# Attention and a squared-ReLU layer on one core: the up-projection by 128-token blocks, with the first loads reordered

## The chip, the cores and the metric

One core of a Trainium2 chip (trn2). The metric is the device time of the whole program in microseconds. Every experiment was timed in several rounds beside the kernel before, on the same chip; the three groups of experiments ran on three chips. "Ratio" is always the mean time of one kernel's fast runs over that of the other's fast runs of the same rounds, with a 95% interval, so it isn't quite the ratio of the medians that are quoted. Executions over 1.5% slower than the fastest of the same kernel are left out of the means.

## The reference

```python
# q, k, v: (batch 8, heads 8, seq 576, dim 64), fp32; w_in (512, 2048), w_out (2048, 512)
scores = q @ k^T / 8                       # per head
mask   = (rel >= 0) & (rel < 128)          # rel = query position - key position
scores = where(mask, scores - slope[h] * |rel|, -1e9)
attn   = softmax(scores);  x = attn @ v    # x: (4608 tokens, 512)
h = x @ w_in;  g = relu(h) ** 2
out = g @ w_out                            # (4608, 512) fp32
```

A query sees only its own block of 128 keys and the one before, so attention is small. The two projections are most of TensorE's work: for each of nine groups of 512 tokens, 16 tiles of h (128 rows of d_ff by 512 tokens) and four output tiles of 128 tokens.

## The kernel before

The kernel is a list of tasks with keys and dependences. A planner in the kernel's own code simulates the engines and fixes in which order every engine takes up its tasks. On the chip, each engine then works in that fixed order and waits on what isn't there yet. A block of tokens goes: load k, q, v (cast to bf16 by GpSimd's DMA), turn k and q (TensorE transposes at first, DMA transposes later), scores, exponentials, mix with v, turn x, then h for whole groups of 512 tokens.

```python
# the planner: when does a load count as landed?
            if t.dma is not None:
                at = max(st + dur + 900.0, self.dma_free)
                self.dma_free = at + t.dma
                t.end = self.dma_free + 900.0
...
    # b: k, q, v of a block; i: a quarter of w_in; o: a quarter of w_out
    FIRST = "b0 b1 b2 b3 b4 i0 i1 i2 i3 b5 b6 b7 b8 b9 o0 o1 o2 o3"
    SPLIT = [(0, 512)]
    KQ_DMA, X_DMA = 10, 13      # from which block on k/q and x are turned by DMA
    size = {"kq": 4, "v": 6, "kqT": 5, "P": 3, "x": 3}     # rings of buffers
...
    def fc_step(g, fc, key, lo=0, hi=512):       # one 128-row tile of h
        ...
        for cc in range(C):                      # C = 4 slices of d_model
                nc.tensor.matmul(slot.tile[:, 0:w], w_in_sb[:, cc, fc * 128:(fc + 1) * 128],
                                 xT[:, cc, g * 512 + lo:g * 512 + hi], start=cc == 0, stop=cc == C - 1)
            # depends on t_win[fc // 4] and on the x of all tokens lo..hi
        ... # ScalarE: relu;  VectorE: square into g
    def t_part(g, t, part, key):                 # 128 output tokens, 4 of 16 slices of d_ff
        ...
                nc.tensor.matmul(slot.tile, sg.tile[:, fc, t * 128:(t + 1) * 128], w_out_sb[:, fc, :],
                                 start=fc == 0, stop=fc == FCB - 1)
        ... # ScalarE copies the 128x512 tile, SyncE stores it (256 KB)
```

The softmax here doesn't subtract the row's maximum and nothing guards it: scores larger than these inputs give would overflow.

## Time and profile before

| | before |
|---|---|
| time, median of the first three runs | 321.29 us |
| span of the profiled run | 318.9 us |
| TensorE's share of the chain that ended last | 91% |
| first up-projection matmul | 24.05 us |
| last matmul ends | 315.07 us |
| from there to the end of the span | 3.83 us |

How to read it: TensorE is the bound nearly everywhere, so the idle time of the other engines costs nothing by itself. What can be had is at the start, where TensorE has nothing to do until loads have landed, and at the end, where the last tile is copied and stored. The prediction below shows the lines.

### The profile page before, as it was taken

Reading aid. Unit: us, or ns where it says so; the run is one execution under the profiler, and the core shown is the slowest. Engines: PE = TensorE matmul, PEld = TensorE weight load, DVE = VectorE, ACT = ScalarE, POOL = GpSimd, SP = SyncE. Lnnn points to the kernel's source line nnn. Section 1 sums busy time; section 2 is a strip of 40 time slices with the busy share of each in tenths; the row PEclk is TensorE's granted clock in tenths of the full one; section 3 lists DMA queues with packets and bytes.
Section 4 is the critical chain, followed back from the end, with each engine's and each line's share of the span. In section 5 each row is a group of like instructions: output and inputs, shape, how many; then the busy total and the mean of one; then the engine's idle time right before and its main releaser. Section 6 shows DMA issues by size and latency. Waiting matters only on the chain.

```text
span 318.9 us, 6368 instructions
## 1 busy us (share of the span) xinstructions
PE 303.5 (95%) x2436; PEld 154.0 (48%) x2436; DVE 166.9 (52%) x476; ACT 176.2 (55%) x330; POOL 107.3 (34%) x133
## 2 busy tenths in 40 slices
PE   2779999999999999999999999999999999999995
PEld 1654555455555545444444454444544454444442
DVE  4782786367468655555545565555545563222200
ACT  4654874476386764555655573555655563444311
POOL 8974956157436336233442334221100000000000
PEclk9997999999999999999999999999999999999999
DMA  9999999999999999989997999996921111000121
GB/s 69 146 183 175 170 201 160 180 137 178 192 156 136 176 186 160 175 115 134 151 168 103 118 121 149 169 117 99 143 56 52 49 51 42 35 33 33 44 90 66
DMA packets 166783, 39.22 MB, mean 123 GB/s; under 512 B 158048, under 2 KB 162144, under 8 KB 166752
## 3 DMA queue, kind: packets, MB, share of 16 engines
q0 software_dynamic: 116736, 18.36, 85.4%
q1 hardware_dynamic: 50016, 20.46, 32.2%
q8 instruction: 19, 0.31, 0.4%
q14 instruction: 12, 0.10, 0.1%
HBM read 36.70 MB, written 9.44 MB: 145 GB/s over the span
## 4 chain that ended last, share of the span: by engine, by line
PE 91%; DMA 3%; DVE 2%; POOL 1%; issue 1%; ACT 1%; POOLq 0%; ACTq 0%
PE h L506 39%; PE o L535 39%; PE ps_s L370 6%; PE pv L419 5%; DMA xT<-x 2%; PE tp L326 1%; DMA kq<-in_q_dram 1%; PE xp L466 1%; POOL kq L284 1%; DVE x L447 1%; DVE P L397 1%; DVE kqT L298 1%; ACT kqT L300 0%; DVE xT L298 0%; POOL vt L284 0%
## 5 line engine op out<-in xcount | busy, mean ns | idle before, releaser
L506 PE MATMUL h<-xT,w_in_sb 128*128 128x512 bf16 x576 | 148.3, 382 | 1.1 <-DMA xT<-x 0.6
L535 PE MATMUL o<-w_out_sb,g 128*128 128x512 bf16 x576 | 147.2, 379 | 0.0
L515 ACT ACTIVATE rt<-h 128x512 bf16<-128x512 f32 x144 | 86.1, 605 | 97.7 <-PE h L506 92.5
L521 DVE TENSOR_TENSOR g<-rt 128x512 bf16<-128x512 bf16 x144 | 60.3, 420 | 83.9 <-ACT rt L515 82.8
L506 PEld LDWEIGHTS <-w_in_sb 128*128 128x128 bf16 x576 | 53.6, 98 | 59.8 <-issue 3.9
L535 PEld LDWEIGHTS <-g 128*128 128x128 bf16 x576 | 52.5, 98 | 56.4
L389 ACT ACTIVATE P<-ps_s 128x512 bf16<-128x512 f32 (+1 forms) x132 | 68.1, 593 | 13.8 <-PE ps_s L370 13.7
L284 POOL DMA_DIRECT2D kq<-in_k_dram x40 | 34.3, 859 | 70.3 <-DMA kqT<-kq 65.0
L284 POOL DMA_DIRECT2D vt<-in_v_dram x40 | 34.2, 858 | 47.8 <-PE pv L419 31.0
L397 DVE TENSOR_TENSOR P<-P,masks 128x512 bf16<-128x512 bf16 (+1 forms) x104 | 42.2, 411 | 14.7 <-ACT P L389 10.5
L419 PEld LDWEIGHTS <-P 128*128 128x128 bf16 x576 | 27.9, 99 | 17.5 <-DVE P L397 1.3
L284 POOL DMA_DIRECT2D kq<-in_q_dram x40 | 34.2, 856 | 3.4 <-PE h L506 1.7
L447 DVE TENSOR_TENSOR x<-pv,rec 128x256 bf16<-128x256 f32 (+1 forms) x80 | 33.2, 419 | 1.7
L546 ACT ACTIVATE osb<-o 128x512 f32<-128x512 f32 x36 | 21.6, 599 | 19.2 <-PE o L535 19.2
L419 PE MATMUL pv<-vt,P 128*128 128x65 bf16 x576 | 31.1, 195 | 0.7 <-DVE P L397 0.3
L442 DVE RECIPROCAL rec<-pv 128x4 f32<-128x4 f32 (+1 forms) x80 | 14.1, 179 | 18.2 <-PE pv L419 15.9
L370 PEld LDWEIGHTS <-kqT 64*128 64x128 bf16 x576 | 15.8, 97 | 14.9 <-issue 12.5
L370 PE MATMUL ps_s<-kqT 64*128 64x128 bf16 (+1 forms) x320 | 19.5, 218 | 0.8 <-DVE kqT L298 0.8
L370 PE MATMUL ps_s<-kqT,kqT 64*128 64x128 bf16 (+1 forms) x256 | 18.8, 217 | 1.1 <-DVE kqT L298 1.1
L326 PE MATMUL tp<-ident,kq 128*128 128x128 bf16 x80 | 8.4, 255 | 6.6 <-DMA kq<-in_k_dram 5.0
L397 DVE TENSOR_TENSOR P<-P,pair_masks 128x512 bf16<-128x512 bf16 x28 | 11.8, 424 | 5.3 <-ACT P L389 3.9
L326 PEld LDWEIGHTS <-kq 128*128 128x128 bf16 x80 | 6.2, 115 | 8.2 <-DMA kq<-in_k_dram 5.3
(25 smaller groups left out, 39.4 us busy)
## 6 DMA issues: line engine op xcount, KB each, us to landing
out_dram<-osb SPq DMA_DIRECT2D x36, 256.0 KB, 2.7
kq<-in_k_dram POOLq DMA_DIRECT2D x32, 128.0 KB, 5.4
kq<-in_q_dram POOLq DMA_DIRECT2D x32, 128.0 KB, 5.8
vt<-in_v_dram POOLq DMA_DIRECT2D x32, 128.0 KB, 5.8
w_in_sb<-in_moe_w_in_dram POOLq DMA_DIRECT2D x4, 512.0 KB, 9.9
w_out_sb<-in_moe_w_out_dram POOLq DMA_DIRECT2D x4, 512.0 KB, 10.1
kq<-in_k_dram POOLq DMA_DIRECT2D x8, 64.0 KB, 3.7
kq<-in_q_dram POOLq DMA_DIRECT2D x8, 64.0 KB, 4.1
```

The source lines that it names most:

```text
L284: nc.gpsimd.dma_start(o, src[b, :, kb * 128:kb * 128 + n, :].rearrange("h s d -> s h d"))
L326: nc.tensor.transpose(slot.tile[:, i * 128:(i + 1) * 128], kq[s_in[m, "k"].idx][:, i // C, (i % C) * 128:(i % C + 1) * 128], ident)
L370: nc.tensor.matmul(slot_s[2 * (c // 2) + half].tile.rearrange("p (c x) -> p c x", c=2)[:, c % 2, at:at + w], kqT[sk_of[mk].idx][rows, c, : ...
L389: nc.scalar.activation(Pv(i), view(slot_s[i].tile.rearrange("p (c x) -> p c x", c=2)), AF.Exp, bias=0.0, scale=scale)
L397: nc.vector.tensor_tensor(pt, pt, view(mk), op=ALU.mult)
L419: nc.tensor.matmul(slot_v.tile[:, hi * (D + 1):(hi + 1) * (D + 1)], Pt[sP.idx][:, place(h)].rearrange("p t q -> p (t q)")[:, at_of[m, part ...
L447: nc.vector.tensor_tensor(xt[sx.idx][0:n, hf * 256:(hf + 1) * 256].rearrange("p (h e) -> p h e", h=4), pv[0:n, :, 0:D], srec.tile[0:n, :]. ...
L506: nc.tensor.matmul(slot.tile[:, 0:w], w_in_sb[:, cc, fc * 128:(fc + 1) * 128], xT[:, cc, g * 512 + lo:g * 512 + hi], start=cc == 0, stop=c ...
L515: nc.scalar.activation(srt.tile[:, 0:w], slot.tile[:, 0:w], AF.Relu, bias=0.0, scale=1.0)
L521: nc.vector.tensor_tensor(sg.tile[:, fc, lo:hi], srt.tile[:, 0:w], srt.tile[:, 0:w], op=ALU.mult)
L535: nc.tensor.matmul(slot.tile, sg.tile[:, fc, t * 128:(t + 1) * 128], w_out_sb[:, fc, :], start=fc == 0, stop=fc == FCB - 1)
L546: nc.scalar.activation(so.tile, slot.tile, AF.Copy)
```

## The change

Its intent: h of the first 512 tokens no longer waits for all five blocks of the first batch. It is computed block by block (128 tokens), so its work can begin when one block of x and the first quarter of w_in are there, and the loads are put in the order in which that work wants them. The first k and q come as fp32 through SyncE's queue beside GpSimd's casting loads. Sixteen dummy matmuls at the start and 36 in planned waits are to keep TensorE's clock up. The very last output tile is made as 384 and 128 columns, so that its last copy and store are smaller. Rings of buffers were resized, and the planner learns that a queue holds eight loads at most.

```diff
         def avail(t):
             at = t.ready
+            if t.dma is not None or t.engs.get("SP"):
+                e = next(iter(t.engs))
+                if len(lanes[e]) >= 8:
+                    at = max(at, lanes[e][-8])
...
-    FIRST = "b0 b1 b2 b3 b4 i0 i1 i2 i3 b5 b6 b7 b8 b9 o0 o1 o2 o3"
-    SPLIT = [(0, 512)]
-
-    KQ_DMA, X_DMA = 10, 13
+    FIRST = "b0 b1 i0 b2 i1 b3 i2 b4 o0 i3 o1 b5 b6 o2 o3 b7 b8 b9"
+    SPLIT = {0: [(0, 128), (128, 256), (256, 384), (384, 512)], 1: [(0, 192), (192, 512)]}
+    EARLY = 0
+    AHEAD = {10: 90, 1: 60, 4: 90, 9: -30, 5: -30, 0: 60, 12: 90, 11: 0, 2: 0, 8: -60, 7: 30, 6: -30, 3: 90}
+    LEAD = 20
+
+    KQ_DMA, X_DMA = 9, 13
+    WARM = 16
+    FILL, UNTIL = 0.5, 26e3
...
-    size = {"kq": 4, "v": 6, "kqT": 5, "P": 3, "x": 3}
+    size = {"kq": 4, "v": 7, "kqT": 4, "P": 2, "x": 4}
...
+    def warm():
+        for i in range(WARM):
+            nc.tensor.matmul(bank(sw)[:, 0:128], zero, zero, start=True, stop=True)
...
+        wide = m == 0
+            if wide and nm != "v":
+                    nc.sync.dma_start(kq32[:, i]..., src[b, :, kb * 128:kb * 128 + n, :]...)   # fp32
...
+        for fi, fc in enumerate(fcs):          # as many 128-row tiles of h as fill a bank
+            for cc in range(C):
+                    nc.tensor.matmul(bank(slot)[:, fi * w:(fi + 1) * w], w_in_sb[:, cc, fc * 128:(fc + 1) * 128],
+                                     xT[:, cc, g * 512 + lo:g * 512 + hi], start=cc == 0, stop=cc == C - 1)
...
+    LAST = [(0, 384), (384, 512)]              # the last tile: ScalarE copies the first, VectorE the second
...
-    done = plan.order()
+    done = fill(plan.order())                  # puts dummies into planned waits of TensorE
```

## The prediction

> **What bounds the kernel now.** I read the page first (busy table, 40 slices, chain of waits), then the stretches of one microsecond for the first 32 us, then the chain in order of time and the timeline, for the start and for the end.
>
> ```profile
> PE   2779999999999999999999999999999999999995
> PEclk9997999999999999999999999999999999999999
> GB/s 69 146 183 175 170 201 160 180 137 178 192 156 136 176 186 160 175 115 134 151 168 103 118 121 149 169 117 99 143 56 52 49 51 42 35 33 33 44 90 66
> ...
> PE 91%; DMA 3%; DVE 2%; POOL 1%; issue 1%; ACT 1%; POOLq 0%; ACTq 0%
> PE h L506 39%; PE o L535 39%; PE ps_s L370 6%; PE pv L419 5%; DMA xT<-x 2%; PE tp L326 1%; DMA kq<-in_q_dram 1%; PE xp L466 1%; POOL kq L284 1%; DVE x L447 1%; DVE P L397 1%; DVE kqT L298 1%; ACT kqT L300 0%; DVE xT L298 0%; POOL vt L284 0%
> ```
>
> TensorE is the bound: 91% of the chain. Only the first three slices (8 us each) and the last are not full. So the time can only fall by TensorE work done earlier in the first 24 us, by less work, or by a shorter end.
>
> ```profile
> 4.79 0.61 PE L326 MATMUL tp<-ident,kq 128*128 128x128 bf16 x4 [4.79 <-DMA kq<-in_k_dram]
> ...
> 14.34 3.10 POOL L259 DMA_DIRECT2D w_in_sb<-in_moe_w_in_dram  x4
> ...
> 22.06 0.88 POOL L284 DMA_DIRECT2D kq<-in_q_dram  x1 [1.11 <-DMA w_in_sb<-in_moe_w_in_dram]
> ...
> 24.05 8.07 PE L506 MATMUL h<-xT,w_in_sb 128*128 128x512 bf16 x29 [0.52 <-DVE xT L298]
> ```
>
> The first k tile lands at 4.8 us. All five blocks of the first batch are loaded before any weight, and the up-projection h begins at 24.05, when all 512 tokens of its group are ready.
>
> ```profile
> 8.00:9.00 1.00, 0.74 (x8) 0.35 (x4) 1.00 (x2) 1.00 (x4) 1.00 (x3) 1.00 2.29 146
> ...
> 16.00:17.00 1.00, 1.00 (x15) 1.00 (x13) 0.69 (x3) 0.86 (x2) 1.00 (x2) 1.00 1.12 83
> ...
> 20.00:21.00 1.00, 0.47 (x4) 0.23 (x4) 1.00 (x3) 1.00 (x3) 0.95 (x2) 1.00 1.25 204
> ...
> 25.00:26.00 1.00, 1.00 (x4) 0.30 (x3) 0.00 (x0) 0.05 (x1) 0.49 (x1) 0.50 1.25 209
> ```
>
> The columns are PE, PEld, DVE, ACT, POOL, granted clock, DMA share, GB/s. The transfers never rest: 146 to 152 GB/s in block loads, 204 to 209 in weights (the drop to 83 is the change from one to the other). At 24 to 27.4 us the clock is 0.5, after an idle spell.
>
> ```profile
> 14.65 1.03 PE ps_s L370 x16
> ...
> 24.05 8.07 PE h L506 x29
> 32.12 0.45 PE tp L326 x8
> ```
>
> 29 up-projection matmuls took 8.07 us; at 0.86 us for four, the rate later, they would take 6.2. Sixteen score matmuls took 1.03 us at 14.65 and 0.55 us later: TensorE ran at half speed there too, though the clock column says 1.00.
>
> ```profile
> 309.73 5.34 PE L535 MATMUL o<-w_out_sb,g 128*128 128x512 bf16 x24
> ...
> 315.16 0.60 ACT L546 ACTIVATE osb<-o 128x512 f32<-128x512 f32 x1 [2.86 <-PE o L535]
> ```
>
> The end is 3.83 us after the last matmul (315.07): copy 0.60, issue 0.33, landing 2.0, the rest closing.
>
> **What the Trainium skill says.** "TensorE: Matmul & The Clock Gate", Part 1: the array starts at half clock and gets the full one after a window of about 3.4 us of activity, and loses it after an idle one. The trace agrees: half speed to about 18 us and again from 24 to 27.4. Same page, Back-to-back issue gap: N/2.4 + 2.5 ns, so 56 ns for 128 columns and 216 for 512. The trace agrees, with weights loaded for each: 0.45 us for eight transposes, 0.86 for four h. So cutting 512 tokens into four pieces costs only 4 x 56 - 216 = 8 ns per matmul. "DMA: Bandwidth & Descriptors", SWDGE vs HWDGE vs iDMA: only the GpSimd path casts; SyncE's issue in hardware, without a cast. That is why the first k and q now come as fp32 through SyncE. No run here shows yet how fast those land.
>
> **The change, part by part.**
>
> *Transfers.* Per load of 128 tokens I take 131 KB / 149 GB/s = 0.88 us; per weight quarter 524 KB / 205 GB/s = 2.55 us. Weights count as landed 2.0 us after their last byte: the bytes of the first quarter are complete at 19.6 (sum of the stretches), and it lands 7.2 us after its issue at 14.34, so at 21.5. In the changed kernel GpSimd first makes the iota (0.38 from 1.25), then issues v0, k1, q1, v1 (0.93 each, to 5.35). Before, the first load had its bytes 1.8 us after its issue ended, so v1 is complete at 7.1; k0 and q0 run beside. From there the transfers are the limit, in the new order (i: w_in quarter, o: w_out quarter, b: block): i0 9.7, b2 12.3, i1 14.9, b3 17.5, i2 20.1, b4 21.4, o0 24.0, i3 26.5, o1 29.1, b5 31.7, b6 34.3, o2 36.9, o3 39.4. Landed: i0 11.7, i1 16.9, i2 22.1, o0 26.0, i3 28.5, o1 31.1, o2 38.9, o3 41.4.
>
> *TensorE from i2 on.* In the instruction order as built, 64 of the 256 small h matmuls stand ahead of the first that needs i2. From it to the last output matmul that waited for o3 there are 192 h x 56 ns = 10.75 us, 32 output matmuls x 216 = 6.9, three blocks of transposes 1.35, two score bursts 1.1, pv of block 3 0.5, two x transposes 0.45: 21.1 us, so 22.1 + 21.1 = 43.2. The waits on the way fall where work is just done: i3 28.5 against 28.8, o1 31.1 against 31.1, o3 + 8 x 216 ns = 43.1.
>
> *Compared with before.* At 44.85 before had all of h for group 0, one output matmul, 72 transposes, scores and pv to block 6. At 43.2 the changed one has 31 output matmuls more (6.7 us). It lacks 40 pv matmuls (at 0.24 us per eight, 1.2), 12 x transposes (0.67), and 16 k/q transposes, of which 8 are saved by turning block 9 by DMA (net 0.45). The split of group 1 adds 0.16 (64 x 2.5 ns). It is ahead by 6.7 - 2.5 = 4.2 us in work and 1.65 in time: 5.85 us.
>
> *The dummies* (16, and 36 in waits) lie in idle time. They may warm the clock earlier; the slack ahead of i1 and i2 (about 1.5 us each) hides most of what a cold clock costs there. I give them no sum of their own.
>
> *The end.* The last 128 columns are copied by VectorE: the row with 128x256 from PSUM takes 0.42, so about 0.25 instead of 0.60; and a quarter of the bytes should land about 0.4 sooner (256 KB moved in two slices of 0.47 us). 16 more matmuls add 0.04. Sum 0.7.
>
> *Taken off:* 0.5 us for small waits from the just-in-time order and ScalarE's share. Total 5.85 + 0.7 - 0.5 = 6.05; 321.29 - 6.05 = 315.2.
>
> **The rivals.** (1) TensorE is in order, and one late weight or block holds all that stands behind it. The arrivals agree within 0.3 us, so there is no slack after 22 us: every microsecond of delay on the transfers is lost one for one. If the fp32 loads through SyncE and the casting loads slow each other, i2 lands 2 us late: 317.2. (2) ScalarE: about 30 instructions at 0.5 us spacing in those 21 us, some 15 us. With two h buffers, a burst of four exponentials can hold h; up to 2 us: 317. (3) The transfers are hidden anyway and later loads take the gain back: against it, GpSimd waits 65 us for freed kq buffers, so loads are held by buffers, not by rate. But there are fewer kqT (5 to 4) and P (3 to 2) buffers, and a wait can appear where before had a single one of 0.6 us. Worth 0 to 2 us. (4) Better than summed: k0 lands early and the dummies hold the clock, so the work ahead of i1 and i2 is never late, and the new order avoids part of the 4.5 us that before loses between 44.85 and 315.07 over the bare sum of its matmuls (265.7): 312.5.
>
> **Range and chances.** The sum of 6.05 us is 1.9%, on the edge of 2% (6.4 us). The start term has an error of about 2 us either way, the later part 1 us. Range 312.3 to 318.3. Faster by over 2%: 0.43; within 2%: 0.54; slower: 0.03, since nothing adds TensorE work that could cost 6 us.
>
> **What would show it.** Right: the first h at about 12.6 us instead of 24; i0, i1, i2 landing near 11.7, 16.9, 22.1; TensorE full from 22 us; the run of eight output matmuls that waits for o3 ending near 43; the end 3.1 us after the last matmul; clock at full speed from about 18 us on without a second drop. Wrong: waits of TensorE for w_in or w_out of over 1 us after 22 us (rival 1), h waiting for ScalarE (rival 2), new waits after 45 us (rival 3), or a second spell of half clock.

## The result, and the profile after

| | before | changed |
|---|---|---|
| median (runs) | 321.01 us (4) | 317.39 us (4) |
| lowest to highest | 320.21 to 321.85 | 315.45 to 317.58 |
| ratio, 95% interval | | 0.9873 (0.9827 to 0.992) |
| span of the profiled run | 318.9 | 313.7 |
| last matmul ends | 315.07 | 310.37 |
| from there to the end | 3.83 | 3.33 |

The changed kernel is about 4 us faster, 1.3%: within 2%. The profiled run, at 315.45 us, is the fastest of its four, and that matters for what follows. First, TensorE's row and its clock of the changed kernel's page, and the chain that ended last.

```profile
PE   7789999999999999999999999999999999999995
PEclk9999999999999999999999999999999999999999
...
PE 83%; DMA 12%; POOL 3%; issue 1%; DVE 0%; DVEq 0%
```

The second clock drop of the kernel before is gone and the third slice is fuller. The chain has more DMA (12% against 3%) although the kernel is faster: the chain now passes through loads that TensorE only just waits for. So the share of DMA in a chain isn't the loss.

Next, TensorE's timeline of the changed kernel: start, duration, operation, and in brackets how long it sat idle and on what.

```profile
12.48 0.89 PE L580 MATMUL hs<-xT,w_in_sb 128*128 128x128 bf16 x13
...
22.20 0.23 PE L580 MATMUL hs<-xT,w_in_sb 128*128 128x128 bf16 x1 [0.31 <-DMA w_in_sb<-in_moe_w_in_dram]
...
29.46 0.73 PE L580 MATMUL hs<-xT,w_in_sb 128*128 128x128 bf16 x10 [0.21 <-DMA w_in_sb<-in_moe_w_in_dram]
```

The first h is at 12.48 us instead of 24.05. At 22.20 TensorE takes up the first h that needs the third quarter of w_in (i2), after a wait of 0.31 us. The run of output matmuls that waits for the last quarter of w_out ends at 44.35:

```profile
40.52 3.83 PE L631 MATMUL os<-w_out_sb,g 128*128 128x512 bf16 x16
```

The end of the same kernel:

```profile
310.07 1.03 SPq L618 DMA_DIRECT2D out_dram<-osb  x2
310.45 0.29 DVE L612 COPY osb<-os 128x128 f32<-128x128 f32 x1 [13.72 <-PE os L631]
```

VectorE's copy of the last 128 columns takes 0.29 us, where ScalarE's of 512 took 0.60, and the 64 KB store lands in 1.6 us where 256 KB took 2.0.

### The profile page after: what moved, and what is told of

Read it like the earlier page. It is cut to its first block, busy times and chain, and to the rows that moved or that the text cites. A ratio compares the mean times of both kernels' runs of the same rounds, so it can differ in the third digit from the quotient of the medians.

```text
span 313.7 us, 6983 instructions
## 1 busy us (share of the span) xinstructions
PE 301.0 (96%) x2711; PEld 170.2 (54%) x2752; DVE 166.7 (53%) x483; ACT 178.9 (57%) x339; POOL 105.9 (34%) x131
## 4 chain that ended last, share of the span: by engine, by line
PE 83%; DMA 12%; POOL 3%; issue 1%; DVE 0%; DVEq 0%
PE os L631 37%; PE hs L580 35%; DMA w_in_sb<-in_moe_w_in_dram 6%; PE as L445 5%; PE as L492 4%; DMA kqT<-kq 3%; DMA xT<-x 2%; POOL kq L332 1%; POOL vt L332 1%; PE at L401 1%; PE at L538 0%; POOL w_out_sb L307 0%; POOL w_in_sb L300 0%; PE os L492 0%; DVE osb L612 0%
## 5 line engine op out<-in xcount | busy, mean ns | idle before, releaser
L580 PE MATMUL hs<-xT,w_in_sb 128*128 128x512 bf16 (+3 forms) x810 | 148.9, 312 | 3.1 <-issue 1.4
L631 PE MATMUL os<-w_out_sb,g 128*128 128x512 bf16 (+2 forms) x573 | 144.3, 373 | 1.2 <-issue 0.2
L589 ACT ACTIVATE rt<-hs 128x512 bf16<-128x512 f32 (+2 forms) x152 | 86.8, 582 | 85.3 <-PE hs L580 72.9
L596 DVE TENSOR_TENSOR g<-rt 128x512 bf16<-128x512 bf16 (+2 forms) x152 | 61.6, 405 | 74.2 <-ACT rt L589 73.0
L464 ACT ACTIVATE P<-as 128x512 bf16<-128x512 f32 (+1 forms) x132 | 69.1, 589 | 17.7 <-PE as L445 17.4
L332 POOL DMA_DIRECT2D vt<-in_v_dram x40 | 34.4, 863 | 16.9 <-PE as L492 10.7
L610 ACT ACTIVATE osb<-os 128x512 f32<-128x512 f32 (+1 forms) x36 | 21.5, 598 | 20.7 <-PE os L631 20.7
L520 DVE TENSOR_TENSOR x<-as,rec 128x256 bf16<-128x256 f32 (+1 forms) x70 | 28.9, 418 | 1.2
L492 PE MATMUL as<-vt,P 128*128 128x65 bf16 x504 | 25.8, 193 | 0.0
L445 PE MATMUL as<-kqT,kqT 64*128 64x128 bf16 (+1 forms) x256 | 17.9, 212 | 2.0 <-ACT kqT L351 1.4
L445 PE MATMUL as<-kqT 64*128 64x128 bf16 (+1 forms) x320 | 18.8, 213 | 0.7 <-DMA kqT<-kq 0.5
```

The costliest lines, as they stand in the source:

```text
L332: nc.gpsimd.dma_start(o, src[b, :, kb * 128:kb * 128 + n, :].rearrange("h s d -> s h d"))
L445: nc.tensor.matmul(slot_s[2 * (c // 2) + half].tile.rearrange("p (c x) -> p c x", c=2)[:, c % 2, at:at + w], kqT[sk_of[mk].idx][rows, c, : ...
L464: nc.scalar.activation(Pv(i), view(slot_s[i].tile.rearrange("p (c x) -> p c x", c=2)), AF.Exp, bias=0.0, scale=scale)
L492: nc.tensor.matmul(bank(slot_v)[:, hi * (D + 1):(hi + 1) * (D + 1)], Pt[sP.idx][:, place(h)].rearrange("p t q -> p (t q)")[:, at_of[m, par ...
L520: nc.vector.tensor_tensor(xt[sx.idx][0:n, hf * 256:(hf + 1) * 256].rearrange("p (h e) -> p h e", h=4), pv[0:n, :, 0:D], srec.tile[0:n, :]. ...
L580: nc.tensor.matmul(bank(slot)[:, fi * w:(fi + 1) * w], w_in_sb[:, cc, fc * 128:(fc + 1) * 128], xT[:, cc, g * 512 + lo:g * 512 + hi], star ...
```

## The experiments

My theory after the result: (A) the gain is made at the start, where the order of loads and the split belong together; the time follows the landing of the weights, one for one, and i2 (the third w_in quarter) above all; the rest is the smaller last store. Rivals: (B) the dummies' clock makes the gain; (C) the later part, by rings or order, gives some back.

### The changed kernel again

No edit; more runs and a second trace.

> The changed kernel, unchanged, to see its spread: its first four times were 315.45 (the profiled one) and 317.3 to 317.6, 2 us apart, where the kernel before keeps within 1.6. Theory A (the phase of the TensorE clock): the times again fall into two groups about 2 us apart near 315.5 and 317.5, and if the profile falls on a slow one, the half-speed spell ends later than the 8.0 us seen so far, and everything after it is later by as much. Theory B (the transfers): in a slow run the w_in and w_out quarters land about 2 us later than at 12.3, 17.3, 22.2 and 29.4 us, with the clock change at the same place.

Measured: 316.23 us median, 315.17 to 317.47 in six runs, ratio 0.9863 (0.9835 to 0.9891). Of all ten runs of the changed kernel, four lie at 315.2 to 315.6 and six at 316.8 to 317.6. The profiled run (316.81, span 315.0) was of the upper kind. GpSimd's timeline of the first profile, then of this one, where it issues i2:

```profile
11.12 0.92 POOL L332 DMA_DIRECT2D vt<-in_v_dram  x1
11.99 0.81 POOL L300 DMA_DIRECT2D w_in_sb<-in_moe_w_in_dram  x1
```

```profile
11.12 0.92 POOL L332 DMA_DIRECT2D vt<-in_v_dram  x1
12.94 0.76 POOL L300 DMA_DIRECT2D w_in_sb<-in_moe_w_in_dram  x1 [0.90 <-DMA w_in_sb<-in_moe_w_in_dram]
```

Everything on GpSimd up to 11.12 us is alike to 0.01 us, but here GpSimd then sat 0.90 us until an earlier w_in quarter had landed. That quarter is i0: i0 and the seven loads behind it were still open, and the ninth waits for i0. It was issued at 5.05 in both runs, landed 6.3 us later in the first and 7.6 in this one. TensorE on this run:

```profile
23.26 0.23 PE L580 MATMUL hs<-xT,w_in_sb 128*128 128x128 bf16 x1 [0.71 <-DMA w_in_sb<-in_moe_w_in_dram]
```

So i2 was 1.06 us later, and the run of output matmuls that waits for the last w_out quarter ended at 45.05, 0.7 later than in the first profile. It would be easy to take this for the first part of the 1.3 us between the two spans. But by 65 us this run was only 0.07 us behind, and it lost the 1.3 us near 111 us; the section on the order planned for later landings has the table. Why the same load, issued at the same time, lands 1.3 us later isn't in these traces: both moved about 1440 KB in the first 10 us.

### No dummies

```diff
-    FILL, UNTIL = 0.5, 26e3
+    FILL, UNTIL = 0.0, 26e3
...
-        for i in range(WARM):
+        for i in range(0):
```

> The changed kernel without any of its 52 dummy matmuls, all else in the same order. Prediction's view (dummies lie in idle time, no sum of their own): within 0.5 us of the changed kernel, 317. Theory A (the clock decides): the full clock comes some 3 to 8 us later, at 12 to 17 us instead of 8, the first h matmuls run at half speed, and the time rises by 1.5 to 3 us, to 318.5 to 320.

Measured: 316.20 us (315.43 to 318.00), ratio 0.9862 (0.9834 to 0.9891): the same as with them. They do move the clock: thirteen h matmuls of the first block took 0.89 us in the first profile and 1.57 without dummies. Full speed came at about 8 us with them; without them matmuls of 128 columns still followed each other by 107 ns up to 16.7 us (but for 0.4 us near 15), and the full rate is there from 17.7. But all that work stands ahead of i1 and i2, which it has to wait for anyway. Rival B falls: the dummies are worth nothing here. This run's profile was of the upper kind again (span 316.2), and again i2 was late:

```profile
13.60 0.76 POOL L300 DMA_DIRECT2D w_in_sb<-in_moe_w_in_dram  x1 [1.56 <-DMA w_in_sb<-in_moe_w_in_dram]
```

i0 took 8.3 us to land, so i2 was issued at 13.60 and used at 24.22. Three profiles with i2 at 22.20, 23.26 and 24.22 have spans of 313.7, 315.0 and 316.2. That looks like one for one, but is so only in part: of the 2.5 us of the third, 1.06 were there at 65 us, and 1.46 were added near 111.

### The kernel before with the last tile in two parts

```diff
-                nc.tensor.matmul(slot.tile, ..., w_out_sb[:, fc, :],
+                nc.tensor.matmul(slot.tile[:, lo:hi], ..., w_out_sb[:, fc, lo:hi],
+            put(slot, lo, hi, last, {"ACT": act(hi - lo)})            # columns 0 to 384
+            if final: ... put(slot, 384, 512, last, {"DVE": dve(128)})
```

> The kernel before with one part of the change alone: the last tile's output in 384 and 128 columns. From the traces the end after the last matmul went from 3.83 to 3.33 us: 0.5 us faster than before, 320.5 against 321.0. If the gain of the end is in truth given back by the 16 more matmuls: 0.

Measured: 319.67 us against 320.49 for before, ratio 0.9966 (0.9942 to 0.999). The medians say 0.8 us, the ratio 1.1, and the two profiles of the main comparison 0.5; in this run's own profile the end after the last matmul was 3.0 us instead of 3.83. It is a sure but small part.

### Whole groups with the new order of loads

```diff
-    SPLIT = {0: [(0, 128), (128, 256), (256, 384), (384, 512)], 1: [(0, 192), (192, 512)]}
+    SPLIT = {}
```

> The changed kernel with the up-projection again by 512 tokens (both groups), all else kept: new order of loads, dummies, two stores. If the block split is what lets the work start early: h starts only when block 3 has its xT, at about 25 us; the early gain of 4.2 us goes and the slow clock may return after the idle spell, so 320 to 323. If the order of the loads alone carries the gain: 317 to 318.

Measured: 325.70 us (324.87 to 327.00), ratio 1.0158 (1.0131 to 1.0185): 5 us slower than before. Clock line of its page, and one stretch (columns: window, length, then PE, PEld, DVE, ACT, POOL with instruction counts, clock, DMA share, GB/s):

```profile
PEclk9979999999999999999999999999999999999999
```

```profile
20.00:24.00 4.00, 3.19 (x42) 2.75 (x41) 1.09 (x4) 1.58 (x4) 2.37 (x3) 0.59 1.61 186
```

The first h comes at 28.77 us, later than before's 24.05: the weights stand in front of blocks that a whole group needs. TensorE is busy only 2.03 of the 4 us from 16 to 20 us, and then its clock falls to 0.59, seen as the 7 in the third slice. (The tile offsets in this run stay those that were searched with the split.)

### The old order of loads with the split, and the new order without it

```diff
-    FIRST = "b0 b1 i0 b2 i1 b3 i2 b4 o0 i3 o1 b5 b6 o2 o3 b7 b8 b9"
+    FIRST = "b0 b1 b2 b3 b4 i0 i1 i2 i3 b5 b6 b7 b8 b9 o0 o1 o2 o3"
```

> The changed kernel with the old order of first loads (all five blocks of the first batch, then w_in, five blocks, w_out), block split and the rest kept. Theory C (the split needs the early weights): the first quarter of w_in lands at about 20.5 us, so the 64 small h matmuls (3.6 us) that ran before 22 us are lost against a start at 20.5 instead of 22: 2 us slower than the changed kernel, about 318.3. Rival D (the order of loads is worth nothing, the split alone gives the gain): 316.2, as the changed kernel. Rival E (the order is all of it): 320 or more.

Measured: 318.55 us (317.61 to 321.25) against 321.12, ratio 0.9934 (0.9902 to 0.9967); span 316.6. The first h is at 21.4 us. The reverse edit in the kernel before:

> The kernel before with the new order of first loads alone. If the order helps by itself: under 319.5. If it only pays with the split, as the whole-group run (325.7) suggests: h still begins at 24 to 26 us, the later blocks come behind w_out, and the time is 320 to 325.

Measured: 326.42 us (325.50 to 326.83), ratio 1.0155 (1.0132 to 1.0178). Here the first h is at 30.66.

What follows from the four: the new order alone costs 5 us, the split with all the rest but the old order gives 2.1 (0.66%), of which the smaller last store is 0.8 to 1.1, and both together give 4.1 to 4.4. The order is worth something only to a kernel that can use what it brings. That is the first half of theory A. The planner's rule of eight loads, and the turning of block 9 by DMA, were not tried alone.

### One more load ahead of i2

An unused quarter of weights is loaded on GpSimd's queue just before i2; no result depends on it.

```diff
+            if t is t_win[2]:
+                nc.gpsimd.dma_start(spare, moe_w_in[:, 0:d_ff // 4].rearrange("(c p) f -> p c f", p=128))
             t.emit()
```

> The changed kernel with one load more, a weight quarter into an unused tile, on GpSimd's queue just ahead of the third w_in quarter; the order of the work on every engine is otherwise the same. Rival 1 of the prediction (in-order TensorE, no slack after 22 us): the third quarter and all behind it land 2.55 us later and the time rises by about 2.5 us, to 318.7. If TensorE and not the transfers sets the start: under 1 us, 317.

```profile
25.59 0.23 PE L581 MATMUL hs<-xT,w_in_sb 128*128 128x128 bf16 x1 [3.51 <-DMA w_in_sb<-in_moe_w_in_dram]
25.66 0.55 PE L539 MATMUL ot<-ident,x 128*128 128x128 bf16 x4
26.00 1.06 PE L581 MATMUL hs<-xT,w_in_sb 128*128 128x128 bf16 x8
```

Measured: 320.16 us (319.14 to 321.52) in two clusters, ratio 0.9972 (0.9945 to 0.9999); the profiled run was its fastest, 319.14, span 317.4. In it i2 came 3.39 us later than in the first profile of the changed kernel, the span is 3.7 us longer. Eight h matmuls took 1.06 us after the wait instead of 0.61: the 3.51 us of idleness also cost the clock. I had expected 318.7; the delay was larger than the 2.5 us that a quarter takes (i2 was also issued 1.34 us later, since the added load is one more that is open), and the clock came on top.

### Three loads fewer

The v of blocks 1 to 3 is set to zero by GpSimd instead of loaded. The result is wrong (relative error 0.222); the work of all the other engines stays.

```diff
+                if nm == "v" and m in (1, 2, 3):
+                    nc.gpsimd.memset(o, 0.0)
+                    return
```

> The changed kernel with v of blocks 1 to 3 set to zero by GpSimd in place of three loads (2.6 us of transfers ahead of the third w_in quarter; wrong result on purpose), order of TensorE the same. If the transfers alone set the start: 2.6 us faster, 313.6. If transfers and TensorE are matched as the prediction has it (saturated from the third quarter on, 21.1 us of matmuls): the waits for weights vanish, the spread between runs shrinks, and the gain is under 1.5 us: 315 to 316.

Measured: 314.15 us (313.99 to 314.88), ratio 0.9787 (0.9769 to 0.9806). TensorE's waits in that trace (waiter, releaser: total, times, longest), all of them:

```profile
PE as L448 <- ACT kqT L354: 1.5, 2, 0.9
PE os L387 <- DVE far L237: 1.1, 1, 1.1
PE as L287 <- DVE vt L266: 1.0, 1, 1.0
PE as L448 <- DVE kqT L352: 0.8, 2, 0.6
PE os L387 <- DMA kq<-in_q_dram: 0.5, 1, 0.5
PE ot L541 <- DVE x L523: 0.3, 1, 0.3
```

No wait for a weight is left. The spread shrank from 2.3 us to 0.9. TensorE reached i2's place at 22.58 and ended the run behind the last w_out quarter at 44.36, as the best run of the changed kernel. So when the weights aren't late, TensorE's own work, with its waits for the copies of kqT ahead of i2, sets 44.4, and the landing is no longer one for one below that: fewer bytes don't help further there. But 1.2 us were gained after that point, where I had expected nothing, and with TensorE's order unchanged.

### The order planned for later landings

Where did the later 1.2 us lie? Five traces have the same order of work on TensorE, so the same output tile can be compared in all of them. The table has when ScalarE starts to copy it out, in us ("last" is ScalarE's last).

| output tile | first profile | again | no dummies | three loads fewer | one load more |
|---|---|---|---|---|---|
| 1st | 43.52 | 44.22 | 44.95 | 43.53 | 47.93 |
| 4th | 64.46 | 64.52 | 65.52 | 63.84 | 68.23 |
| 8th | 110.03 | 110.09 | 111.09 | 109.41 | 113.81 |
| 9th | 118.82 | 120.18 | 121.34 | 117.66 | 122.45 |
| last | 309.55 | 310.92 | 312.08 | 308.40 | 313.19 |

The traces part in three places only: before the first tile, where the weights land; between the 1st and the 4th, where the first profile waits 0.5 us for kqT at about 62 us and so loses its lead over the second; and between the 8th and the 9th, where against the run with three loads fewer the others lose 0.5, 1.8, 2.0 and 0.4 us. In this last place TensorE waits for one h, at about 111 us. In the first profile the trace puts the wait (0.5 us) down to xT, in the second it names an exponential:

```profile
112.76 1.04 PE L580 MATMUL hs<-xT,w_in_sb 128*128 128x512 bf16 x3 [0.94 <-ACT P L464]
```

But the transpose of x that this h needs landed at 112.71, 0.05 us before. It is the same in the other traces: landed at 111.35, 113.87 and 114.98, h at 111.39, 113.92 and 115.03. With three loads fewer it landed at 109.94, before TensorE was there, and nothing waited. So it is the landing of this one transpose that makes most of the distance of the second and third profile from the first. Whether it also makes the two clusters of the runs without a trace isn't shown, and why it varies isn't known: in the first two profiles it was issued at 103.64 and 103.71 and took 7.7 and 9.0 us. (The second also has a wait of 0.6 us for kqT there.)

kqT and xT are written there by DMA transposes. The planner counts any DMA as landed 0.9 us after its last byte. In the stretch from 95 to 118 us the x transposes took 6.5 to 7.7 us from issue to landing in the first profile and 6.9 to 9.0 in the second, and the weights' 2 us after the last byte was already in the prediction. So I altered that one constant:

```diff
-                t.end = self.dma_free + 900.0
+                t.end = self.dma_free + 2500.0
```

> The changed kernel with one constant of its own order planner altered: the lag from a load's last byte to the wait it satisfies is taken as 2.5 us and not 0.9 us. No load, copy or store is altered, only in which order TensorE takes up work. Theory (the order is planned for weights that land earlier than they do, and the later short waits for kqT and xT come of that): fewer such waits, 315.5 to 316.0 us, spread under 1.5 us. Rival (TensorE is full, order no longer matters): the changed kernel's own 316.3 us, with its spread of over 2 us.

Measured: 314.59 us (314.19 to 315.69), ratio 0.981 (0.9783 to 0.9837): better than I expected, the spread 1.5 us. Its median is below the lowest of the ten runs of the changed kernel (315.17). The two were not timed in the same rounds nor on the same chip, and the intervals of their ratios just overlap (0.9837 and 0.9835). The trace says where it is. TensorE's waits at 100 to 125 us, changed kernel (second profile), then this one:

```profile
PE hs L580 <- ACT P L464: 0.9, 1, 0.9
PE as L445 <- DMA kqT<-kq: 0.6, 1, 0.6
PE hs L580 <- issue: 0.2, 1, 0.2
```

```profile
PE hs L580 <- issue: 0.3, 2, 0.2
PE os L631 <- issue: 0.2, 1, 0.2
```

And the stretch of 110 to 120 us, in the changed kernel's first profile, its second, and this one (TensorE's busy time comes after the length):

```profile
110.00:120.00 10.00, 9.42 (x85) 4.84 (x86) 5.74 (x17) 5.88 (x12) 5.43 (x7) 1.00 1.86 172
```

```profile
110.00:120.00 10.00, 8.30 (x79) 4.24 (x80) 5.23 (x16) 5.14 (x10) 5.27 (x7) 1.00 2.00 173
```

```profile
110.00:120.00 10.00, 9.79 (x100) 5.11 (x100) 6.38 (x20) 5.37 (x11) 5.58 (x7) 1.00 1.62 177
```

The run behind the last w_out quarter ends at 44.37, as in the changed kernel's best run (44.35). The whole difference between the two profiles (312.6 against 313.7) is made after it, mostly by the waits that are gone: 9.33 of 10 us busy at 60 to 70 us became 9.79, and 9.42 at 110 to 120 became 9.79. In this trace TensorE had no wait for a weight either. That another order removes these waits is shown. The run with three loads fewer removed them too, with the old order, so it is the order together with the landings that makes them: rival C holds in this form. What I expected says that only TensorE's order is altered; in fact all engines are ordered anew: SyncE's stores and transposes change places, and some of GpSimd's loads and some copies too. Which of these matters isn't shown. Dummies are placed into planned waits, so there are 54 instead of 52; the run without dummies says that they don't matter.

### Searched anew for later landings

The same constant, and an order of first loads and tile offsets that the kernel's own planner likes best with it.

```diff
-    FIRST = "b0 b1 i0 b2 i1 b3 i2 b4 o0 i3 o1 b5 b6 o2 o3 b7 b8 b9"
+    FIRST = "b0 b1 b2 i0 b3 i1 i2 b4 o0 o1 o2 i3 b5 o3 b6 b7 b8 b9"
...
-    AHEAD = {10: 90, 1: 60, 4: 90, 9: -30, ...};  LEAD = 20
+    AHEAD = {10: 0, 1: -90, 4: 120, 9: -90, ...};  LEAD = 30
```

> The changed kernel with the same longer lag, and with its order of first loads and its tile offsets searched anew for that lag. Meant to beat both kernels. If the planned order for real landings is worth anything: about 315.6 us, 0.7 us under the changed kernel. Rival: within 0.4 us of 316.3 us, or slower if moving i0 behind a third block of tokens makes the landing of i2 later.

Measured: 314.62 us (313.56 to 315.06), ratio 0.9802 (0.9775 to 0.9829). It beats the kernel before by 2.0%, and is not to be told from the one-constant edit. Its first h comes at 14.53 us, 2 us later than the changed kernel's, with no loss that could be measured: here an early first h was worth nothing by itself.

### The old rings

```diff
-    size = {"kq": 4, "v": 7, "kqT": 4, "P": 2, "x": 4}
+    size = {"kq": 4, "v": 7, "kqT": 5, "P": 3, "x": 4}
```

> The changed kernel with the rings of buffers of kqT and P put back to the sizes they had before (5 and 3). Third rival of the prediction: if the changed ring sizes turn up as the later waits for kqT (0.5 to 0.7 us in three profiles), the old sizes remove them, 315.8 us. Theory that those waits come of the order: 316.3 us, unchanged, within 0.5 us.

Measured: 317.74 us (315.54 to 320.24), ratio 0.991 (0.9866 to 0.9953): not faster than with the smaller rings, and with a wider spread. TensorE's order is the same; one more kqT transpose is issued ahead, and in this trace no wait for kqT is left at 62 or 111 us. So the smaller ring may have its part in those short waits, but not in what costs most. The profiled run (319.79) had a start as good as the best, its run behind the last w_out quarter ending at 44.3, and lost 5 us against the first profile in one place:

```profile
110.01 0.25 PE L445 MATMUL as<-kqT 64*128 64x64 bf16 x4
114.08 1.03 PE L580 MATMUL hs<-xT,w_in_sb 128*128 128x512 bf16 x3 [3.82 <-issue]
```

```profile
110.00:120.00 10.00, 6.13 (x47) 2.92 (x41) 3.28 (x10) 3.26 (x6) 3.94 (x5) 0.83 1.99 169
```

TensorE stood 3.82 us at the h behind a burst of scores, and lost its clock (0.83 over the stretch). The profile names no releaser ("issue"), but it is the same wait, grown long: the transpose of x, issued at 105.73, landed at 113.99, and the h started at 114.08. Whether the larger rings made it later or chance did isn't settled by one trace; in the run below, with the smaller rings, it landed as late as 115.76.

### k and q of the first block through the casting path again

```diff
-        wide = m == 0
+        wide = False
...
-        elif m == 0:
+        elif False:
```

> The changed kernel with k and q of the first tile put back on GpSimd's casting path (narrow loads, bf16 transposes), so SyncE's queue takes no early load. If the two paths together bring the early bytes sooner and the first weights' landing sets the end one for one: first h and i2 later by 1 to 1.5 us, 317.3 to 317.8 us. Rival (SyncE's fp32 loads only take bandwidth from GpSimd's, which carry the critical weights, and cost fp32 transposes): 316.3 us or less.

Measured: 317.75 us median of seven (316.68 to 321.51), ratio of the fast ones 0.9891 (0.9859 to 0.9923). In its trace:

```profile
14.93 0.82 PE L580 MATMUL hs<-xT,w_in_sb 128*128 128x128 bf16 x6 [0.21 <-DMA w_in_sb<-in_moe_w_in_dram]
```

The first h is 2.45 us later, and i2 was used at 25.69. The median is inside what I expected for a one-for-one delay; by ratios the loss is 0.6 to 0.9 us, and the intervals overlap with the changed kernel's. The profiled run (321.27) was 2.9 us behind the first profile from the first output tile to the eighth, and then lost 3.3 more at the same transpose of x (a wait of 1.6 us near 116 us, with a lost clock), so it isn't a clean measure. The numbers lie on the side of the fp32 loads helping, which is not settled.

## Why the prediction was right or wrong

The class (within 2%) and the range held. The time predicted, 315.2, is that of the changed kernel's lower cluster (315.2 to 315.6), and 1 to 2 us under its medians. That it meets the fastest runs so closely is luck in part: 6.05 us were taken off a median of 321.29, while the two profiled runs (320.67 and 315.45) are 5.2 apart. By their spans this is 0.5 us of lead at the start, 4.2 of work and 0.5 at the end, where 1.65, 4.2 and 0.7 were predicted, less 0.5. Point by point:

- **Transfers.** i0, i1, i2 were predicted to land at 11.7, 16.9, 22.1; in the profile of the fastest run it was 11.4, 17.1 and 22.20 (the last as TensorE's wait ended), and the first h came at 12.48 where 12.6 was predicted. The fp32 k and q through SyncE landed 3.3 and 4.0 us after their issue. Up to i2 this step was right for that run; i3 and o1 landed at 29.4 and 31.9, 0.9 and 0.8 later than predicted. And it took one number for what varies: i2 was at 23.26 and 24.22 in two further profiles, because i2's issue waits for i0's landing. I had the queue's eight open loads in the code before me (the new rule in the planner) and didn't ask what it makes of a late i0.
- **TensorE from i2 on, 21.1 us.** Measured from i2's place to the end of the run behind the last w_out quarter: 22.15, 21.8, 21.55 us in the three traces, and 21.8 with fewer loads. The sum of the instructions was 0.5 to 1.0 us short. In the first trace about half of that is TensorE held by the two late quarters, i3 (0.37 us) and o1 (0.18), where the prediction had them land just in time; 0.2 are gaps ahead of the two score bursts, and 0.16 is the tail of the last matmul. This is why the lead at the start was 0.5 us and not 1.65: the step that was too small. No wait of TensorE for an exponential is listed in this stretch.
- **State against before, 4.2 us of work.** Right: the kernel before needed 270.2 us of time from the matching point to the end of its last matmul, the changed one's best run 266.0.
- **The end, 0.7 us.** Measured 0.5 in the two profiles and 0.8 to 1.1 in the run of that part alone.
- **Taken off for small waits, 0.5 us.** Too little as well. Even the best run waited 0.5 us for kqT at 62 us and 0.5 for xT at 111; the second profile lost 1.3 us more than it near 111, and the one without dummies 1.5. Of i2's lateness, 1.06 and 2.0 us, only 0.07 and 1.06 were left at 65 us. Together that is the distance of their spans (315.0 and 316.2) from 313.7.
- **Dummies, no sum.** Right, and shown. Full speed came at about 8 us with them, ten sooner than I wrote, and it didn't matter.
- **Rival 1** (a late weight is lost one for one): held by the load added, 3.4 us later for 3.7 us; but only down to TensorE's own 44.4 us, by the loads taken away, and not always: in the second profile 1.06 us of lateness had become 0.07 by 65 us, because the first profile then waited for a kqT and the second did not. **Rival 2** (h held by ScalarE): not seen; no wait for the relu in the list of the changed kernel. **Rival 3** (later waits): there, at the landings of DMA transposes that the order, planned with a lag of 0.9 us, has too early; the larger rings did not make the kernel faster. **Rival 4** (the new order avoids later losses): not in the changed kernel, and reachable by one constant.
- **What was drawn from the skill.** "TensorE: Matmul & The Clock Gate", Back-to-back issue gap, gives the formula for a single matmul and 81 and 131 ns for a stream of them with weight loads; here such streams ran at 56 and 216 ns, so the formula was the right choice and the measurement decides. The prediction also took from Part 1 of that page that the clock is lost after an idle window; it was lost at 24.0 us in the kernel before after 3.45 us in which TensorE was busy 1.92 us, with no gap over 0.6: a stretch half idle, so the trace agrees with that only loosely.

So of the 6.05 us predicted, 4.1 to 4.4 came (the ratios' 1.27 to 1.37% of 321 us). The rest, some 2 us, is a lead at the start that is a good 1 us smaller than summed, and waits for DMA transposes that land later than the order assumes; the one-constant edit, 1.7 to 2.0 us faster by the ratios, has in its profile all of that at the second.

## What to carry to other kernels

An order of loads and the granularity of the work that uses them are one change: the order alone cost 5 us here, and the finer work without it gave half the gain. When a fixed order comes out of a simulated schedule, check the simulated landing times against the trace; mending one constant that was too hopeful was worth more than the dummies or the ring sizes, and a new search on top added nothing that could be measured. Profile a second run before trusting a landing time: the same load, issued at the same time, landed 2 us apart. And before calling an early delay the cause of a longer time, follow the same piece of work through both traces: the delay may have been made up long before the end.

## What the Trainium skill lacked or had wrong

- "DMA: Bandwidth & Descriptors" has no number of loads that may be open on one issuing queue, and nothing on what the next one costs. Here the ninth load on GpSimd's queue waited for the landing of the first, with GpSimd idle for 0.90 and 1.56 us in two traces. Whether that is the chip's limit or the program's way of counting, no run tells.
- The same page, "Anatomy of one DMA — SWDGE (gpsimd) path", fits a load as 2.0 us and its bytes at 436 GB/s, which makes 3.2 us for a weight quarter of 512 KB (an estimate from that fit). Behind other loads the four w_in quarters of the changed kernel's first profile landed 6.3 to 11.2 us after their issue, and the first of them after 6.3, 7.6 and 8.3 us in three traces. The fit has no term for what stands ahead of a load.
- The same page, "DMA Transpose (X-bar)", has no latency for a transpose among running loads. Here x transposes took 6.5 to 9.0 us from issue to landing, in two profiles of the changed kernel at 95 to 118 us; an order that counted on less made TensorE wait.
- "TensorE: Matmul & The Clock Gate" tells how to get the full clock, but not that it can be worth nothing ahead of a wait for data, as here: 316.20 us without the dummies, 316.23 with them.
- No page has it that the clock column of this profile reads 1.00 where the trace holds no clock record yet: in the kernel before the first record begins at 17.19 us, and sixteen score matmuls took 1.03 us at 14.65 us and 0.55 later.
